# Issuing half of the output stores from GpSimd's queue, gating the token loads later, and planning the order anew, in a fused attention and feed-forward kernel

## The chip, the cores and the metric

The kernel runs on one core of a Trainium2 chip. The metric is the device time of one execution in microseconds (us). The profile's span, from the first to the last recorded instruction, is about 1.8 us shorter than that time. Every run has a state, fast or slow; ratios use fast runs only.

The engines are named as the profile does: PE is TensorE, PEld its weight loads, DVE VectorE, ACT ScalarE, POOL GpSimd, SP SyncE. SPq is SyncE's queue, which here does nothing but start transfers.

## The reference

```python
# attention: batch 4, 8 heads, sequence 768, head dimension 64; 8 global keys, window of 96
scores = q @ k.T / 8 + bias(slope per head, distance)     # masked outside window and globals
a = softmax(scores);  x = a @ v                           # -> 3072 tokens x 512
# feed-forward: d_model 512, d_ff 2048
h = x @ w_in
g = max(h, 0) + log1p(exp(-abs(h)))                       # softplus
out = g @ w_out                                           # 3072 x 512, float32
```

## The kernel before

The kernel cuts the 3072 tokens into 12 windows of 256. Each window's attention feeds a group of the feed-forward part: eight steps "mm1" (x times w_in, 8 matmuls of 128x256 each) and eight steps "mm2" (g times w_out, 4 matmuls of 128x512 each). Attention of later windows is laid between feed-forward steps of earlier ones, so that TensorE never runs dry.

No order is written down. Every piece of work is an operation with a rank; a planner inside the kernel simulates the engines and gives each engine, whenever it is free, the ready operation of lowest rank. A table RANKS shifts single ranks and BASE places whole blocks. The result is a list, and the instructions are then issued in its order:

```python
plan = pl.plan({"pe": 1.3, "dve": 4.5, "act": 2.1, "pool": 3.2, "sp": 0.7, "none": 0.0})
for op in plan:
    op.fn(op)
```

Each engine works through its own part of that list strictly in order, and waits at each entry for its data. The parts that the change touches are the stores, and the place of the token loads (q, k, v of a window, 1.5 MB together) in SyncE's queue:

```python
def store(g, ns):
    osb = state["osb", g, ns]                # 128 x 512 float32, three buffers
    t0 = W * g + P * ns
    nc.sync.dma_start(out[t0 : t0 + P, :], osb[:])
# ... two stores in each of eleven groups:
pl.add(f"store{g}_{ns}", "sp", 0.6, lambda op, g=g, ns=ns: store(g, ns), r + 1.5,
       after=[oc], frees=[(oc, "osb")], dma=(8, 110))
# ... loads of windows 4 to 11, in the plan only after a certain mm2 step:
for w in range(4, NWIN):
    for what, p in (("q", 0), ("k", 1), ("v", 3)):
        for o in loaded[w, what]:
            s = NSLOT * (w - 4) + p - PACE
            o.wait_for(mm2s[divmod(s, NSLOT)] if s >= 0 else landed["out3"])
```

SyncE's queue also carries the transposes of q and k (qT, kT) and of the attention's result (XT), some 1.2 us each. A q cast to bf16 runs on VectorE. The `wait_for` above holds only in the plan; on the chip a load waits for its buffer and its place in the queue.

The softmax here doesn't subtract the row's maximum and nothing guards it: scores larger than these inputs give would overflow.

Of the kernel before, what the change touches and what calls it, by code (L numbers as in the profile page):

```python
# [14 lines left out]


RANKS = {
    "Ck3.0": 33.6, "biasA.0": -11.6, "castv1.1": 17.3, "mm1_1_7.0": -3.6, "mm1_1_4.0": 27,
    "bias71.0": 46.2, "pv51.0": 12.4, "pv60.0": -37.2, "mm2_1_3.0": -35.8, "bias20.0": 10,
    "castv4.2": 2.9, "mm1_0_7.0": 16.2, "castv1.2": -20.8, "mm2_1_1.0": 14.7, "scores7.0": 7.8,  # L20
    "pv10.0": 15.8, "mm2_0_3.0": 15.4, "mm1_2_4.0": -4.3, "bias01.0": -10.4, "castk5.3": 11.8,
    "pv11.0": 13, "castv2.0": 11, "Fq1.0": -2, "castv4.3": -1.1, "mm1_1_2.0": -1.7,
    "sexp0_4.0": -6.9, "mm1_1_0.0": 2.2, "TX5.0": -6.8, "store0_1.0": -7.5, "Dq5.0": 0.9,
    "mm1_1_5.0": 3.1, "mm1_0_0.0": -3.2, "mm1_0_1.0": -3.5, "mm1_2_3.0": 2.6, "castv0.4": 4.3,
    "mm2_1_0.0": 12, "castv2.3": -2.5, "castv3.1": -1.2, "mm2_1_7.0": 3.4, "mm2_0_5.0": 14.2,
    "castv0.7": 8.8, "Dq4.1": -5, "castv0.3": -0.3, "castv0.5": 7.1, "mm1_2_2.0": -1.1,
    "mm2_1_4.0": -0.2, "mm1_0_5.0": -3.9, "castv0.1": -1.7, "castv3.3": -4.4, "castv0.2": -10.6,
    "castk4.1": 0.9,
}
HALVED = "q9 k9 q10 k10 v10 q11 k11 v11".split()  # L30
EARLY, MERGED, T_DMA, X_DMA = 4, 6, 4, 6
SP_ORDER = "Q01 K01 v0a Q23 K23 v0b v1 q2@in1 k2 v2 q3@in2 k3 v3"
POOL_ORDER = "in0@Q23 in1 out0 out1@q2 in2 in3 out2 out3"
PACE = 3
BASE = (-29.49, -25.67, -31.22, -11.48, -6.35, 14.94, 12.5, -27.18, 17.37, 24.12, 29.7, 32.51, 31.67, 35.31)


class Op:
# [206 lines left out]
def kernel(  # L245
# [11 lines left out]
    nc = tc.nc  # L257
    P = nc.NUM_PARTITIONS
# [327 lines left out]
    def mm1(g, p, turn):  # L586
        state["h", g, p] = h_ps[turn]
        hv = h_ps[turn][:].rearrange("p (j t) -> p j t", j=2)
        for j in range(2):
            fb = 2 * p + j  # L590
            for m in range(NM):
                nc.tensor.matmul(  # L592
                    hv[:, j, :],
                    w_in_bf[:, m, fb * P : fb * P + P],
                    XT[:, m, W * g : W * g + W],
                    start=(m == 0),
                    stop=(m == NM - 1),
                )

    def softplus_exp(g, p):  # L600
        e = tile_of(ffn, ("e", g, p // 2), [P, 2, 512], F32)

        nc.scalar.activation(  # L603
            e[:, p % 2, :].rearrange("p (a t r) -> p a r t", a=4, r=2),
            state["h", g, p][:].rearrange("p (a r t) -> p a r t", a=4, r=2),
            AF.Exp,
        )
# [55 lines left out]
        osb = tile_of(ffn, ("osb", g, ns), [P, DM], F32)  # L663
        copy_on[eng](osb[:], src)  # L664

    def store(g, ns):
        osb = state["osb", g, ns]
        t0 = W * g + P * ns
        nc.sync.dma_start(out[t0 : t0 + P, :], osb[:])

    def w_in_slice(s, waits):
        n_in = DFF // NS
# [36 lines left out]
    bias0 = const.tile([P, 2, 4, P], BF16, name="bias0")  # L709
    biasA = const.tile([P, 2, 8, P], BF16, name="biasA")  # L710
# [36 lines left out]
    def base(n):  # L747
        return BASE[n] if n < len(BASE) else 4.0 * n - 13.0

# [4 lines left out]
    def add_load(w, what, rank, after=(), hs=ALL, key=None, waits=()):  # L754
        nonlocal chain
        f = 0.5 if hs != ALL else 1.0
        dur, dma = 0.55 * f + 0.05, (64 * f, 28)
        takes = ((what + "32",),) if hs.start == 0 else ()
        o = chain = pl.add(
            f"load{what}{w}", "sp", dur, lambda op: load(w, what, hs, key, waits), rank,  # L760
            after=[*after, *(landed[x] for x in waits)], behind=[chain], takes=takes, dma=dma,
            slack=2.5 if w >= 4 else 0.0,
        )
        loaded.setdefault((w, what), []).append(o)
        return o
# [13 lines left out]
    def load_rest(w, rank, after=()):  # L779
        for i, what in enumerate("qkv"):  # L780
            for hs, _ in halves if what + str(w) in HALVED else whole:
                add_load(w, what, rank + 0.01 * i, after, hs)
# [36 lines left out]
    for w in range(4, NWIN):  # L819
        load_rest(w, base(2 * w) - 13.87 - PACE)  # L820

# [264 lines left out]
    for g in range(NGRP):  # L1086
        for p in range(NSLOT):
            r = NSLOT * g + p + {0: -1.04, 1: -0.28, 2: 0.38, 3: 1.0, 4: 1.55}.get(g, 0.0)
            m1 = mm1s[g, p] = pl.add(
                f"mm1_{g}_{p}", "pe", 0.875, lambda op, g=g, p=p: mm1(g, p, op.taken[0][1]), r,  # L1090
                after=[xdone[2 * g], xdone[2 * g + 1], landed_in[p * NS // NSLOT]],
                takes=(("H",),),
            )
            ex = pl.add(
                f"sexp{g}_{p}", "act", 0.63, lambda op, g=g, p=p: softplus_exp(g, p), r + 0.5,
                after=[m1], takes=(("e",),) if p % 2 == 0 else (), frees=[(m1, "H")],
            )
            if p % 2 == 1:
                lns[g, p // 2] = pl.add(
                    f"sln{g}_{p // 2}", "act", 1.06,  # L1100
                    lambda op, g=g, p=p: softplus_ln(g, p // 2), r + 0.9, after=[ex, prev_ex],
                    takes=(("g",),) if p == 1 else (), frees=[(prev_ex, "e")],
                )
            prev_ex = ex
        if g == NGRP - 1:
            before = None
            for part, (ns, cols, _) in enumerate(LAST):
                f = (cols.stop - cols.start) / DM
                for chunk in range(4):
                    before = pl.add(  # L1110
                        f"mm2l_{part}_{chunk}", "pe", 0.865 * f,
                        lambda op, part=part, chunk=chunk: mm2_last(part, chunk),
                        1000.0 + 4 * part + chunk,
                        after=[lns[g, chunk]], behind=[before],
                        takes=((LAST[part][2][0],),) if chunk == 0 else (),
                    )
                copies[part] = pl.add(
                    f"outl_{part}", "act" if part == 1 else "dve", 0.69 * f,
                    lambda op, part=part: out_last(op.on, part), 900.0,
                    after=[before], takes=(("osb",),),  # L1120
                )
            break
        for p in range(NSLOT):
            if g == 0:

                mm2s[0, p] = pl.add(
                    f"mm2_0_{p}", "pe", 0.865, lambda op, p=p: mm2_first(p, s_ps[1]), 2.19 * p + 2.01,
                    after=[lns[0, p // 2], landed_out[p * NS // NSLOT]], behind=[mm2s.get((0, p - 1))],
                    takes=(("S1",),) if p == 0 else (),
                )  # L1130
                continue
            ns, c = divmod(p, 4)
            mm2s[g, p] = pl.add(
                f"mm2_{g}_{p}", "pe", 0.865,
                lambda op, g=g, ns=ns, c=c: mm2_one(g, o_ps[:], ns, range(4 * c, 4 * c + 4)),
                NSLOT * (g + 1) + p + (-2.58 if g < 4 else 0.5),
                after=[lns[g, c], landed_out[c]], behind=[mm2s.get((g, p - 1))],
                takes=(("O",),) if c == 0 else (),
            )
        r = 2.6 + NSLOT if g == 0 else NSLOT * (g + 1) + 4.0  # L1140
        for ns in range(2):
            last = NSLOT - 1 if g == 0 or ns else 3
            oc = pl.add(
                f"oc{g}_{ns}", "dve", 0.69,
                lambda op, g=g, ns=ns: out_copy(
                    op.on, g, ns, o_ps[:] if g else o_first(ns, s_ps[1])
                ),
                r - 2.06 + 4 * ns, after=[mm2s[g, last], copies.get((g, 0))], takes=(("osb",),),
                frees=[(mm2s[g, 0], "S1")] * ns if g == 0 else [(mm2s[g, last - 3], "O")],
            )  # L1150
            if ns:
                oc.frees = [*oc.frees, (lns[g, 0], "g")]
            copies[g, ns] = oc
            pl.add(
                f"store{g}_{ns}", "sp", 0.6, lambda op, g=g, ns=ns: store(g, ns), r + 1.5,
                after=[oc], frees=[(oc, "osb")], dma=(8, 110),
            )

# [6 lines that stand above are left out]
# [42 lines left out]
```

## Time and profile before

| | before |
|---|---|
| median time | 219.18 us (218.71 to 219.36, 3 runs) |
| span of the profiled run | 217.1 us |
| TensorE busy / fillers | 208.3 us / 88 matmuls of zeros |
| stores | 23 of 256 KB on SyncE, 2.5 us from issue to landing |

TensorE is the bound. Lines from the costliest groups give line, engine, operation, tiles, shapes, count, then busy time and mean length, then the idle time ahead.

### The profile page before, as it was taken

How to read it: one execution, taken by the hardware profiler on the slowest of the kernel's cores; microseconds unless marked ns; L12 is line 12 of the kernel's file. 1: busy time of each engine (PE TensorE's matmuls, PEld its weight loads, DVE VectorE, ACT ScalarE, POOL GpSimd, SP SyncE). 2: the span in 40 equal slices, each digit the busy share in tenths (PEclk: the TensorE clock that was granted, in tenths of full speed). 3: DMA queues.
4: the chain of work that ended last, by engine and by line, in shares of the span. 5: the costliest groups of instructions: out<-in, count | busy, mean ns of one | idle time of the engine just before them, and what ended most of it. 6: DMA issues, size and time to landing. Idle time of an engine off the chain costs nothing.

```text
span 217.1 us, 5062 instructions
## 1 busy us (share of the span) xinstructions
PE 208.3 (96%) x2031; PEld 146.3 (67%) x2064; DVE 122.7 (57%) x261; ACT 153.7 (71%) x205; POOL 58.2 (27%) x113
## 2 busy tenths in 40 slices
PE   8899989999999999899999999999999999999994
PEld 7677766775766667577767767666766766676643
DVE  6878687278849677773555855545853753110020
ACT  3667859973896769768869669749669669766630
POOL 4652630014834360440441423221700000000000
PEclk9999999999999999999999999999999999999999
DMA  5999999999987977978999977969621211200112
GB/s 185 327 227 205 249 197 196 268 292 294 164 186 192 214 214 145 288 87 177 282 166 266 177 188 170 171 179 276 103 77 48 74 27 51 72 35 13 51 48 97
DMA packets 70583, 36.24 MB, mean 167 GB/s; under 512 B 28448, under 2 KB 67616, under 8 KB 70560
## 3 DMA queue, kind: packets, MB, share of 16 engines
q1 hardware_dynamic: 66192, 31.53, 63.8%
q0 software_dynamic: 4224, 4.19, 12.0%
q8 instruction: 16, 0.26, 0.6%
q10 hardware_dynamic: 144, 0.20, 0.3%
q14 instruction: 7, 0.06, 0.1%
HBM read 27.26 MB, written 6.29 MB: 155 GB/s over the span
## 4 chain that ended last, share of the span: by engine, by line
PE 83%; DMA 5%; DVE 4%; SPq 2%; issue 2%; POOL 1%; ACT 1%; DVEq 0%; POOLq 0%
PE h_ps L592 36%; PE o_ps L620 29%; DMA q<-in_q_dram 5%; PE s_ps L493 5%; PE x_ps L548 4%; PE s_ps L620 3%; PE s_ps L645 3%; DVE vb L402 1%; POOL vb L402 1%; SPq L441 1%; PE h_ps L419 1%; PE o_ps L732 1%; PE h_ps L570 1%; DVE xs L560 1%; SPq L582 1%
## 5 line engine op out<-in xcount | busy, mean ns | idle before, releaser
L592 PE MATMUL h_ps<-XT,w_in_bf 128*128 128x256 bf16 x768 | 96.0, 273 | 0.1
L603 ACT ACTIVATE e<-h_ps 128x512 f32<-128x512 f32 x96 | 58.7, 629 | 38.5 <-PE h_ps L592 38.1
L592 PEld LDWEIGHTS <-w_in_bf 128*128 128x128 bf16 x768 | 73.0, 98 | 19.1
L620 PE MATMUL o_ps<-w_out_bf,g 128*128 128x512 bf16 x294 | 75.5, 379 | 1.8 <-DVE osb L664 0.4
L611 ACT ACTIVATE g<-e 128x1024 bf16<-128x1024 f32 x48 | 50.5, 1055 | 0.6
L620 PEld LDWEIGHTS <-g 128*128 128x128 bf16 x352 | 32.1, 98 | 26.8 <-issue 0.4
L524 DVE TENSOR_TENSOR z<-s_ps,biasA 128x1024 f32<-128x1024 f32 x34 | 40.5, 1220 | 9.4 <-PE s_ps L493 8.0
L530 ACT ACTIVATE pb<-z 128x1024 bf16<-128x1024 f32 (+1 forms) x40 | 39.5, 986 | 7.6 <-DVE z L524 7.4
L402 POOL CAST kb<-k 64x512 bf16<-64x512 f32 x32 | 19.9, 621 | 48.5 <-DMA k<-in_k_dram 47.2
L402 POOL CAST vb<-v 64x512 bf16<-64x512 f32 (+1 forms) x40 | 24.4, 611 | 26.2 <-DMA v<-in_v_dram 24.3
L559 DVE RECIPROCAL rcp<-x_ps 128x4 f32<-128x4 f32 x47 | 8.5, 180 | 37.6 <-PE x_ps L548 34.5
L664 DVE COPY osb<-o_ps 128x512 f32<-128x512 f32 x20 | 13.7, 686 | 22.4 <-PE o_ps L620 22.2
L560 DVE TENSOR_TENSOR xs<-x_ps,rcp 128x256 bf16<-128x256 f32 x47 | 19.9, 424 | 1.7
L548 PEld LDWEIGHTS <-pb 128*128 128x128 bf16 x320 | 14.8, 97 | 3.5 <-issue 1.0
L548 PE MATMUL x_ps<-vb,pb 128*128 128x65 bf16 x312 | 15.8, 193 | 0.9 <-DVE xs L560 0.8
L493 PEld LDWEIGHTS <-kT 64*128 64x128 bf16 x288 | 8.3, 94 | 7.1 <-issue 6.4
L493 PE MATMUL s_ps<-qT,kT 64*128 64x128 bf16 x288 | 12.0, 218 | 0.6 <-DVE z L524 0.6
L471 DVE COPY vb<-vb 4x512 bf16<-4x512 bf16 (+1 forms) x36 | 11.7, 326 | 0.5
L393 DVE CAST qb<-q 128x1024 bf16<-128x1024 f32 x10 | 7.1, 712 | 8.3 <-DMA q<-in_q_dram 8.2
L732 PE MATMUL o_ps<-zeros 128*128 128x128 bf16 x88 | 9.3, 259 | 1.4 <-DVE zeros L687 1.0
L732 PEld LDWEIGHTS <-zeros 128*128 128x128 bf16 x88 | 7.3, 119 | 2.6 <-DVE zeros L687 1.0
L534 ACT ACTIVATE pb<-s_ps 128x1024 bf16<-128x1024 f32 (+1 forms) x8 | 7.3, 918 | 2.2 <-PE s_ps L493 2.2
(74 smaller groups left out, 96.9 us busy)
## 6 DMA issues: line engine op xcount, KB each, us to landing
out_dram<-osb SPq DMA_DIRECT2D x23, 256.0 KB, 2.5
q<-in_q_dram SPq DMA_DIRECT2D x9, 512.0 KB, 4.7
k<-in_k_dram SPq DMA_DIRECT2D x9, 512.0 KB, 6.9
v<-in_v_dram SPq DMA_DIRECT2D x9, 512.0 KB, 7.0
w_in_bf<-in_moe_w_in_dram POOLq DMA_DIRECT2D x4, 512.0 KB, 9.0
w_out_bf<-in_moe_w_out_dram POOLq DMA_DIRECT2D x4, 512.0 KB, 11.4
v<-in_v_dram SPq DMA_DIRECT2D x6, 256.0 KB, 4.5
q<-in_q_dram SPq DMA_DIRECT2D x6, 256.0 KB, 3.4
```

The source lines that it names most:

```text
L402: copy_on[eng](dst[64 * r : 64 * r + 64, hs, :], src)
L493: nc.tensor.matmul(s_t[:, 4 * sub + (lh // 2 if i == 0 else 2 * (lh // 2) + b), :], k_of(n - b, rows, m), q_of(n, rows, m), start=begin, s ...
L524: nc.vector.tensor_tensor(packed(n, z), rows_of(n, s_t), bias, ALU.add)
L530: nc.scalar.activation(pb[:, 0:nr, :], z[:, 0:nr, :], AF.Exp, scale=1.0 / root_d)
L548: nc.tensor.matmul(xv[:, lh, :], pb[:, 2 * j + b, :], vb_of(n - b)[:, h, :], start=b == 0, stop=b == 1,)
L560: nc.vector.tensor_tensor(xs[:, 4 * half : 4 * half + 4, :], xv[:, :, 0:D], rcp[:][:, :, None].to_broadcast([P, 4, D]), ALU.mult,)
L592: nc.tensor.matmul(hv[:, j, :], w_in_bf[:, m, fb * P : fb * P + P], XT[:, m, W * g : W * g + W], start=(m == 0), stop=(m == NM - 1),)
L603: nc.scalar.activation(e[:, p % 2, :].rearrange("p (a t r) -> p a r t", a=4, r=2), state["h", g, p][:].rearrange("p (a r t) -> p a r t", a ...
L611: nc.scalar.activation(gt[:, 4 * c : 4 * c + 4, :].rearrange("p a t -> p (a t)"), state["e", g, c][:].rearrange("p a t -> p (a t)"), AF.Ln ...
L620: nc.tensor.matmul(dst, state["g", g][:, fb, ns * P : ns * P + P], w_out_bf[:, fb, :], start=(fb == 0), stop=(fb == NFB - 1),)
L664: copy_on[eng](osb[:], src)
L732: nc.tensor.matmul(o_ps[:, 0:P], zeros[:], zeros[:])
```

## The change

The intent: twelve of the stores are to leave SyncE's queue, so that they no longer stand ahead of loads and transposes; the loads are gated later; and since the planner's input has changed, ranks and bases were searched anew.

```diff
 RANKS = {
-    "Ck3.0": 33.6, "biasA.0": -11.6, "castv1.1": 17.3, "mm1_1_7.0": -3.6, "mm1_1_4.0": 27,
-    ... (51 entries)
+    "mm1_1_4.0": 26.1, "bias71.0": 63.7, "bias20.0": 9.6, "castk5.3": 11.8, "Dq5.0": 0.9,
+    ... (43 entries)
 }
-HALVED = "q9 k9 q10 k10 v10 q11 k11 v11".split()
+HALVED = "q8 k8 v8 q9 k9 v9 q10 k10 v10 q11 k11 v11".split()
-PACE = 3
-BASE = (-29.49, -25.67, -31.22, -11.48, -6.35, 14.94, 12.5, -27.18, ...)
+PACE = 0
+STORES = 6
+BASE = (-29.37, -38.43, -34.65, -17.24, 5.3, 14.23, -7.79, -35.22, ...)
...
-    def store(g, ns):
+    def store(eng, g, ns):
         osb = state["osb", g, ns]
         t0 = W * g + P * ns
-        nc.sync.dma_start(out[t0 : t0 + P, :], osb[:])
+        start = nc.gpsimd.dma_start if eng == "pool" else nc.sync.dma_start
+        start(out[t0 : t0 + P, :], osb[:])
...
-                f"store{g}_{ns}", "sp", 0.6, lambda op, g=g, ns=ns: store(g, ns), r + 1.5,
+                f"store{g}_{ns}", *(("pool", 0.8) if g < STORES else ("sp", 0.6)),
+                lambda op, g=g, ns=ns: store(op.on, g, ns), r + 1.5,
```

## The prediction

> **What bounds the kernel now.** I read the busy table and the slice chart first, then the table of stretches, then the list of waits of TensorE, then the chain of waits in order of time around the largest hole.
>
> ```profile
> PE 208.3 (96%) x2031; PEld 146.3 (67%) x2064; DVE 122.7 (57%) x261; ACT 153.7 (71%) x205; POOL 58.2 (27%) x113
> ...
> PEclk9999999999999999999999999999999999999999
> ```
>
> TensorE is busy 208.3 of 217.1 us at full clock; the next engine, ScalarE, has 71%. So TensorE is the bound, and the time can fall only by what TensorE idles or wastes: 217.1 - 208.3 = 8.8 us. Where that idle time lies is in the table of stretches (columns: stretch, length, busy time and count of TensorE, weight loads, VectorE, ScalarE, GpSimd, then granted clock, DMA share, GB/s):
>
> ```profile
> 0.00:25.00 25.00, 22.61 (x296) 18.03 (x301) 18.83 (x68) 16.37 (x23) 11.40 (x31) 1.00 1.02 245
> 25.00:75.00 50.00, 49.00 (x490) 34.41 (x497) 34.11 (x64) 37.36 (x51) 16.55 (x28) 1.00 1.13 221
> 75.00:90.00 15.00, 13.60 (x153) 9.92 (x153) 10.95 (x20) 12.03 (x16) 4.51 (x9) 1.00 0.82 204
> 90.00:210.00 120.00, 118.94 (x1063) 81.26 (x1081) 57.84 (x109) 87.50 (x117) 25.71 (x48) 1.00 0.59 129
> 210.00:217.10 7.10, 4.10 (x35) 2.64 (x33) 0.98 (x2) 0.48 (x1) 0.00 (x0) 1.00 0.21 74
> ```
>
> Length minus busy gives the idle time: 2.39 us in the first 25 us (first loads), 1.00 from 25 to 75, 1.40 from 75 to 90, 1.06 over the long regular part, 3.00 at the end (last copies and stores). The start and end hang on the first loads and the last store. Ahead of 90 us the list of waits names three real stalls:
>
> ```profile
> PE x_ps L548 <- DVE xs L560: 0.8, 1, 0.8
> PE s_ps L493 <- DVE z L524: 0.6, 1, 0.6
> PE o_ps L620 <- DVE osb L664: 0.4, 1, 0.4
> ```
>
> They sum to 1.8 us, each one event. The largest, at 89 us, is followed back in the chain of waits in order of time (start, length, what):
>
> ```profile
> 80.10 1.22 SPq L582
> ...
> 81.41 1.75 SPq L441
> ...
> 83.22 4.57 DMA q<-in_q_dram
> ...
> 88.49 0.19 DVE rcp L559
> ```
>
> SyncE worked through transposes, only then issued the q load at 83.22; the load took 4.57 us; VectorE, which takes its work in order, stood before the q cast until 87.8, so the softmax division behind it came late, and TensorE's probabilities-times-V matmuls waited 0.80 us. Why the queue was late shows in SyncE's own timeline and waits:
>
> ```profile
> 69.01 4.02 SPq L441 DMA_TRANSPOSE qT<-qb  x1
> 73.08 1.54 SPq L669 DMA_DIRECT2D out_dram<-osb  x3
> ```
>
> ```profile
> SPq L669 <- DVE osb L664: 31.4, 11, 6.5
> ```
>
> Three stores stood ahead of those transposes for 1.54 us, and over the whole run SyncE stood 31.4 us in 11 waits for a store's result to be copied out of PSUM. Everything behind waited too.
>
> **What the Trainium skill says.** "DMA: Bandwidth & Descriptors", section "Issuing engines are not separate DMA queues": all queues end on the same 16 engines, and another issuing engine "will only save the time on the sequencer it takes to initiate the DMA". The trace agrees as far as it goes: the weight loads of GpSimd's queue took 9.0 to 11.4 us to land while SyncE's loads ran too. So I expect no bandwidth from the move, only SyncE's time. The same page, "Anatomy of one DMA — SWDGE (gpsimd) path", fits a GpSimd DMA as 2.0 us + bytes/436e3; for 256 KB that is an estimate of 2.6 us, beside a median of 2.5 us that SyncE's stores took. Landing time is therefore no reason for or against. "Perfetto Trace Analysis", section "DMA Instruction — SWDGE (GPSIMD)", says that the recorded end of such an issue is the end of descriptor writing, not of the transfer; the trace has these rows at 747 to 926 ns, on GpSimd itself. "SBUF — State Buffer", section "SBUF: two separate sides", warns that VectorE operations in a two-port mode keep GpSimd from writing descriptors; no row of this trace isolates that, though a v cast of 0.61 us median once took 0.96 us.
>
> **The change part by part.**
> 1. Twelve of 22 whole-tile stores leave SyncE. Recorded issues there run from 0.33 to 1.72 us, median 0.377: 12 x 0.38 = 4.5 us of issue, plus a good part of the 31.4 us of waiting. None of it lies on TensorE directly; it counts only where a transpose or load behind it is late, and in this trace that is the 0.80 us stall, perhaps the 0.4 us one (a copy into osb that held TensorE's next output group).
> 2. GpSimd gains them: 12 x 0.82 us (median of its eight weight loads) = 9.8 us as an upper estimate, since a store has 128 rows and a weight slice 512. GpSimd idles 73% of the span, so there is room; but its queue is in order too. A store that waits for osb holds the next k or v casts, and casts that wait for a load hold the store (the longest such wait now is 15.2 us).
> 3. The gate is three steps later. In the built instruction streams the loads wait only for earlier DMA lanes and free buffers, not for the matmul step. The gate is thus only a place in SyncE's order. It puts the loads after more transposes; a load issued at 83.22 that was already late could get later. Against that, between the v load of window 6 and the q load of window 7 the streams have ten other SyncE entries before (three of them stores) and six after. At roughly 1.2 us per transpose and 0.5 us per store that is 1.5 to 3 us sooner, relative to its neighbours, more than the 0.80 us stall.
> 4. The new order. Comparing the streams, TensorE's matmuls are the same 1976 in both apart from fillers, 88 before and 84 after; the order differs mainly before the fifth group, and later little. Four fillers at about 56 ns spacing are 0.2 us. The q, k, v loads of window 8 and v of window 9 are now halved, which lets casts start sooner but adds four issues.
>
> Sum: 1.8 us of named stalls plus 0.2 us of fillers is at most 2.0 us to gain. I chose to credit three quarters of the stalls, 1.35 us, because the order was searched for exactly this, plus the 0.2, and take off 0.1 us for a new short wait: 219.18 - 1.35 - 0.2 + 0.1 = 217.7 us. That is a gain of 0.7%.
>
> **Rivals.**
> - *Hidden anyway.* SyncE's freed time is slack and only one stall hung on it; the reordering moves the others about. For it: the regular part from 90 to 210 us has just 1.06 us of idle in spite of all those SyncE waits. Then 218.6 to 219.4 us. This is the closest rival.
> - *GpSimd becomes the late one.* A store waiting for osb delays k casts, then the k transposes, then scores, and TensorE stalls. For it: GpSimd is already in the chain (four v casts at 76.7 to 79.3 us lead to the late transposes), and the stores come right there. Against it: 58.2 + 9.8 us is 31% of the span, and most casts wait for a load rather than for GpSimd. If two or three windows each lose half a microsecond, 219.5 to 221 us.
> - *Loads late.* The later gate makes q casts on VectorE wait longer; each microsecond of such waiting in the dense part costs up to as much. With one or two events like the one at 88 us: plus 0.8 to 1.6 us, again about 219 to 220.5.
> - *The start improves too.* If the first groups start earlier, part of the 2.39 us of idle and 84 x 56 ns = 4.7 us of fillers in the first 25 us goes. The first 81 fillers stand in the same places in both streams and the first loads are unchanged, so I allow 0.5 us at most: 217.2.
>
> **Range and chances.** All stalls gone and a little of the start gives about 216.3; a gain wholly given back and a new stall gives 219.5. Over 2% faster means below 214.8, a gain of 4.4 us: more than double the stalls named, so 2%. Over 2% slower means 4.4 us of new TensorE idle, which needs a repeated stall in each window: 3%. Within 2%: 95%.
>
> **What would show it.** Right: SyncE's waits for osb fall from 31.4 us to under half; GpSimd shows twelve store issues of at most 0.9 us; idle TensorE from 75 to 90 us falls from 1.40 to below 0.8; the regular part stays near 1.06; the stores' landing stays near 2.5 us. Wrong: new entries in TensorE's waits that lead back through a k or v cast to a store on GpSimd, or through a q cast to a late load; or the same work with TensorE's stalls merely moved. It would also be wrong if the startup changed by over 1 us, which I gave no credit.

## More of the kernel before

```profile
L620 PE MATMUL o_ps<-w_out_bf,g 128*128 128x512 bf16 x294 | 75.5, 379 | 1.8 <-DVE osb L664 0.4
L620 PEld LDWEIGHTS <-g 128*128 128x128 bf16 x352 | 32.1, 98 | 26.8 <-issue 0.4
```

Every matmul has a weight load of its own. There are 352 loads, yet only 294 matmuls are recorded into o_ps and another 28 into s_ps: 30 records are missing (33 over all kinds). Where the record of a matmul is missing, the trace shows idle time.

## The result, and the profile after

The changed kernel took 217.91 us (median of 4 runs, 217.75 to 218.05) beside 219.27 us (4 runs) before. The ratio is 0.9941, with a 95% interval of 0.9919 to 0.9963. A ratio here is the mean time of one kernel's fast runs over the mean of the other's in the same rounds, so it is not quite the ratio of the medians.

The page and the table of stretches after, the counterparts of those in the prediction (same columns; the last stretch ends with the span):

```profile
PE 210.3 (97%) x2060; PEld 146.1 (68%) x2060; DVE 122.0 (56%) x258; ACT 156.4 (72%) x208; POOL 65.2 (30%) x125
```

```profile
0.00:25.00 25.00, 22.32 (x291) 17.60 (x292) 19.03 (x67) 15.58 (x21) 11.23 (x31) 1.00 1.03 245
25.00:75.00 50.00, 49.92 (x497) 34.35 (x495) 33.33 (x61) 40.69 (x55) 18.16 (x31) 1.00 1.10 233
75.00:90.00 15.00, 15.00 (x164) 10.56 (x162) 10.45 (x19) 12.27 (x17) 6.89 (x12) 1.00 0.90 167
90.00:210.00 120.00, 120.00 (x1092) 81.50 (x1089) 58.64 (x112) 87.43 (x116) 28.97 (x52) 1.00 0.54 129
210.00:216.00 6.00, 3.05 (x30) 2.05 (x27) 0.58 (x2) 0.48 (x1) 0.00 (x0) 1.00 0.25 87
```

From 75 to 90 us TensorE is now busy throughout, where it idled 1.40 us. But look at the first line and at the fourth, the regular stretch. In the first 25 us it is busy 22.32 us, 0.29 us less than before. And in the regular stretch it has gone from 118.94 to 120.00 us busy, though both kernels do the same there. The count of matmul records explains the fourth line: 2060 of 2060 this time, none missing, against 2031 of 2064. The 1.06 us are 20 gaps of 0.05 us each, and a later profile of the changed kernel itself (the first control of experiment 7), with 34 records missing, shows 20 such gaps again, 1.16 us. So the 1.06 us that the prediction read as idle was no idle time at all.

Busy time is thus a poor yardstick between these two traces. The weight loads are complete in both, so I use them: **lost time** at a moment is the elapsed time minus the back-to-back time of all real matmuls whose weights have been loaded by then (spacings read off in unstalled stretches: 0.1093 us for 128x256, 0.2158 for 128x512, 0.1625 for 128x384, 0.109 for the 128x256 bias, 0.056 for a 128x128 transpose, 0.035 for a scores matmul, 0.030 for a 65-column one; fillers count as nothing). The real work sums to 197.7 us in both kernels.

| lost time at | 10 us | 25 us | 35 us | 75 us | 90 us | 210 us |
|---|---|---|---|---|---|---|
| before | 7.76 | 11.29 | 12.46 | 13.13 | 14.90 | 16.24 |
| after | 8.03 | 12.20 | 12.53 | 13.59 | 13.84 | 15.16 |
| after minus before | +0.27 | +0.91 | +0.07 | +0.46 | -1.06 | -1.08 |

The steps are good to some 0.2 us, the length of a matmul. The final difference, 1.08 us, agrees with the spans (217.1 - 216.0 = 1.1 us). By stretches: the start to 25 us **loses** 0.91 us, 25 to 75 us gains 0.45 us, 75 to 90 us gains 1.52 us, and the rest nothing. The gain from 25 to 75 us lies all before 35 us (0.84 us), where the stall of 0.6 us stood (at 30.64 us); from 35 to 75 us the changed kernel loses 0.39 us more than the other, and no single wait in its list explains that.

The waits of TensorE after, in full apart from those under 0.5 us:

```profile
PE o_ps L732 <- DVE zeros L687: 1.0, 1, 1.0
PE h_ps L591 <- DVE rcp L558: 0.7, 1, 0.7
PE o_ps L732 <- ACT k_first L385: 0.5, 1, 0.5
```

The first and the last were there before. All three stalls that the prediction names are gone, and there is a new one of 0.7 us: the first feed-forward matmuls, near 18.6 us.

What freed the stage near 89 us is in the list of waits of the other engines. First before, then after (what waited, for what: us in total, times, longest):

```profile
DVE qb L393 <- DMA q<-in_q_dram: 8.2, 4, 4.1
POOL kb L402 <- DMA k<-in_k_dram: 47.2, 7, 10.3
```

```profile
DVE qb L392 <- DMA q<-in_q_dram: 1.4, 1, 1.4
POOL kb L401 <- DMA k<-in_k_dram: 13.7, 5, 5.8
POOL out_dram L669 <- DVE osb L663: 16.8, 6, 6.7
SPq L669 <- DVE osb L663: 27.1, 8, 6.5
```

VectorE stood 8.2 us at q casts whose load had not landed; now 1.4 us. (One q cast moved to GpSimd, where it waits 8.7 us; no wait of TensorE in this profile follows from it.) SyncE's own time at stores hardly fell, from 31.4 to 27.1 us: most of it belongs to the late groups, whose stores still go through SyncE. The list of SyncE's waits before, up to 133 us (the twelve stores that move) and from there on, shows it:

```profile
SPq L669 <- DVE osb L664: 2.6, 3, 1.1
SPq L669 <- DVE osb L664: 28.8, 8, 6.5
```

So the move could save 2.6 us of this waiting at most. And SyncE's timeline after, in the same place as the one that the prediction shows:

```profile
79.98 1.22 SPq L440 DMA_TRANSPOSE kT<-kb  x1
81.25 0.57 SPq L350 DMA_DIRECT2D q<-in_q_dram  x1
```

The q load of window 7 leaves at 81.25 us, 2.0 us sooner than before, and its cast is planned behind other work of VectorE (it runs at 88.82 us, when the data is there). The q load of window 6 left later than before, at 67.72 in place of 66.40 us, as the later gate would have it, and no stall followed.

The stores themselves, from the issues (KB each, median us from issue to landing) and from the source line (ns minimum/median/maximum of the issue):

```profile
out_dram<-osb POOLq DMA_DIRECT2D x12, 256.0 KB, 4.5
out_dram<-osb SPq DMA_DIRECT2D x11, 256.0 KB, 2.1
```

```profile
L669 POOL DMA_DIRECT2D out_dram<-osb x12: 540/542/822, 50.0 to 131.5; - x12
```

They cost GpSimd 0.54 us each, and take twice as long to land as those that SyncE issues. But the two sets do not run at the same time of the kernel. Taken alone, the same twelve stores had a median of 4.2 us on SyncE in the kernel before, and 3.8 and 3.5 us on SyncE in the changed kernel's order (experiment 2); on GpSimd in that order it is 4.5, 4.1 and 5.0 us in three profiles (means: 4.1 us in both on SyncE, 4.3 to 4.5 us on GpSimd). So most of the difference between 4.5 and 2.1 us is the part of the kernel in which they run, and not the queue.

### The profile page after: what moved, and what is told of

The parts are those of the page before. It is cut to its first block, busy times and chain, and to the rows that moved or that the text cites. A ratio compares the mean times of both kernels' runs of the same rounds, so it can differ in the third digit from the quotient of the medians.

```text
span 216.0 us, 5102 instructions
## 1 busy us (share of the span) xinstructions
PE 210.3 (97%) x2060; PEld 146.1 (68%) x2060; DVE 122.0 (56%) x258; ACT 156.4 (72%) x208; POOL 65.2 (30%) x125
## 4 chain that ended last, share of the span: by engine, by line
PE 91%; DMA 3%; DVE 2%; ACT 1%; SPq 1%; issue 0%
PE h_ps L591 40%; PE o_ps L619 32%; PE s_ps L492 6%; PE x_ps L547 5%; DMA q<-in_q_dram 3%; PE s_ps L644 3%; PE s_ps L619 3%; PE o_ps L732 1%; PE h_ps L418 1%; PE s_ps L477 1%; DVE vb L401 1%; DVE kb L370 0%; SPq L358 0%; PE o_ps L644 0%; PE x_ps L544 0%
## 5 line engine op out<-in xcount | busy, mean ns | idle before, releaser
L619 PE MATMUL o_ps<-w_out_bf,g 128*128 128x512 bf16 x320 | 79.6, 379 | 0.0
L401 POOL CAST vb<-v 64x512 bf16<-64x512 f32 (+1 forms) x39 | 23.4, 601 | 5.9 <-DMA v<-in_v_dram 3.9
L401 POOL CAST kb<-k 64x512 bf16<-64x512 f32 x32 | 20.6, 644 | 15.0 <-DMA k<-in_k_dram 13.7
L461 POOL COPY kT<-kT 128x32 bf16<-128x32 bf16 x12 | 2.5, 209 | 36.2 <-PE s_ps L492 26.7
L669 POOL DMA_DIRECT2D out_dram<-osb x12 | 6.8, 568 | 18.7 <-DVE osb L663 16.8
L732 PE MATMUL o_ps<-zeros 128*128 128x128 bf16 x84 | 8.7, 261 | 1.4 <-DVE zeros L687 1.0
```

Source lines behind the costliest of these rows:

```text
L401: copy_on[eng](dst[64 * r : 64 * r + 64, hs, :], src)
L619: nc.tensor.matmul(dst, state["g", g][:, fb, ns * P : ns * P + P], w_out_bf[:, fb, :], start=(fb == 0), stop=(fb == NFB - 1),)
```

## The experiments

Two kinds of run have to be told apart. Changing a constant makes the planner plan everything anew, so such a run changes the order everywhere. To hold the order still, I edited the finished list instead, or only the engine that issues; then every compute engine keeps its order to the instruction (checked on the built streams, and the traces agree). Times are medians of six runs, with the ratio to the kernel before and its 95% interval.

**1. The queue alone.** The order before, stores of six groups from GpSimd.

```diff
     def store(g, ns):
-        nc.sync.dma_start(out[t0 : t0 + P, :], osb[:])
+        start = nc.gpsimd.dma_start if g < 6 else nc.sync.dma_start
+        start(out[t0 : t0 + P, :], osb[:])
```

> The order of the kernel before is kept instruction for instruction on every engine; only the twelve stores of the first six groups go out through GpSimd's queue in place of SyncE's. Theory Q (SyncE's queue): the stores ahead of the transposes made the window-7 q load late, so the 0.8 us stall near 89 us goes and perhaps the 0.4 us one near 77: 218.0 to 218.6 us, q load issued 1.5 to 2 us sooner than 83.2. Rival O (order): the queue alone buys nothing, 219.0 to 219.5 us, and the three stalls of TensorE stay. Rival G (GpSimd late): stores hold k casts, over 219.8 us.

218.88 us, ratio 0.9987 (0.9966 to 1.0008): no clear gain, just under the range that the rival O gave. The trace shows both theories half right. SyncE's q load of window 7 left at 81.26 us, and the stall near 89 us shrank: lost time rose by 0.26 us from 80 to 90 us, against 1.23 us before. But a new wait took its place:

```profile
PE s_ps L493 <- DMA qT<-qb: 1.3, 1, 1.3
```

The chain of waits in order of time, ahead of it, and GpSimd's timeline there:

```profile
67.36 1.33 SPq L351
...
68.73 9.18 DMA qT<-qb
...
78.05 0.63 PE s_ps L493 x16
```

```profile
68.51 1.60 POOL L670 DMA_DIRECT2D out_dram<-osb  x3 [0.32 <-issue]
```

A q transpose stands right behind the three loads of window 6 (1.5 MB) in SyncE's queue. Three stores (768 KB) now start on GpSimd at 68.5 us, at the same moment; in the kernel before they stood behind the transpose, at 73.08 us. The transpose lands 9.18 us after issue and TensorE waits 1.3 us. In the kernel before the same transpose was issued at 69.01 us, landed after 7.17 us, and the same scores ran at 76.69 us without a wait. The v load just ahead of the transpose was slowed as much: it landed after 10.09 us in place of 8.06.

**2. The order alone.** The changed kernel's order, all stores from SyncE, tried on two chips (the second time beside the changed kernel).

```diff
-        start = nc.gpsimd.dma_start if eng == "pool" else nc.sync.dma_start
+        start = nc.sync.dma_start
```

> The order of the changed kernel is kept on every engine; only the twelve stores go back to SyncE's queue, at the places where the plan has them. Theory Q: the late loads come back, 218.6 to 219.4 us. Rival O: the time stays at 217.8 to 218.2 us, that is the new order alone makes the gain and the queue is irrelevant.

> The changed kernel's order with all stores back on SyncE, again, now beside the changed kernel. In the first trial its profiled run lost no more TensorE time than the changed kernel, yet its six runs spread over 1.5 us (218.18 to 219.72). If the queue move buys steadiness: again a spread over 1 us and a mean 0.5 to 1.2 us above the changed kernel of this batch. If that spread was chance: within 0.3 us of the changed kernel.

First 218.79 us, ratio 0.9989 (0.9963 to 1.0014); then 218.87 us, ratio 0.9977 (0.9948 to 1.0006), with a mean 0.59 us above the changed kernel of the same batch. So the order alone is not the gain either. The profile of the first trial was one of its better executions (218.38 us) and lost no more TensorE time than the changed kernel. That of the second (219.44 us) shows what the stores do in SyncE's queue:

```profile
65.67 0.53 SPq L669 DMA_DIRECT2D out_dram<-osb  x1
66.29 2.54 SPq L440 DMA_TRANSPOSE kT<-kb  x2
68.88 1.26 SPq L440 DMA_TRANSPOSE qT<-qb  x1
70.20 1.42 SPq L350 DMA_DIRECT2D q<-in_q_dram  x1
```

The q load of window 6 leaves at 70.20 us; in the changed kernel it left at 67.72 us. VectorE and TensorE, in their timelines:

```profile
75.76 0.70 DVE L392 CAST qb<-q 128x1024 bf16<-128x1024 f32 x1 [2.19 <-DMA q<-in_q_dram]
```

```profile
77.05 0.40 PE L547 MATMUL x_ps<-vb,pb 128*128 128x65 bf16 x8 [0.96 <-DVE xs L559]
```

VectorE stands 2.19 us before the q cast and TensorE loses 0.96 us. It is the mechanism of the old stall at 89 us, one window earlier. The expectation that the queue move would buy steadiness fell: the changed kernel itself spread over 1.45 us in that batch (217.61 to 219.06).

**3. One late load alone.** The kernel before, stores on SyncE, with the q load of window 7 five transposes sooner in SyncE's queue, and nothing else moved; tried twice.

```diff
+    i = next(k for k, op in enumerate(plan) if op.name == "loadq7")
+    j = next(k for k, op in enumerate(plan) if op.name == "castq6")
+    j = max(j, next(k for k, op in enumerate(plan) if op.name == "store1_1"))
+    ... (a print)
+    plan.insert(j + 1, plan.pop(i))
     for op in plan:
         op.fn(op)
```

> The kernel before with one thing moved: the q load of window 7 stands five transposes sooner in SyncE's queue, the stores stay where they are. If the late q load is the cause of the largest stall (TensorE 0.8 us near 89 us, 1.06 us of lost work there): the stall is gone and the time is 218.1 to 218.5 us. If VectorE's order or the transposes are the cause, the stall stays or moves and the time is 219.0 to 219.6 us.

> The kernel before with the q load of window 7 five transposes sooner, again. If that one late load is what the whole change amounts to: 0.5 to 1.1 us below the kernel before, within 0.4 us of the changed kernel. If the changed kernel's other differences count: 0.5 us or more above the changed kernel.

First 218.36 us, ratio 0.9973 (0.9948 to 0.9998); then 218.49 us, ratio 0.9957 (0.9924 to 0.9991). VectorE's q cast in the kernel before:

```profile
87.88 0.69 DVE L393 CAST qb<-q 128x1024 bf16<-128x1024 f32 x1 [1.21 <-DMA q<-in_q_dram]
```

In the first trial, SyncE's q load and then VectorE:

```profile
75.96 0.58 SPq L351 DMA_DIRECT2D q<-in_q_dram  x1
```

```profile
86.60 0.68 DVE L393 CAST qb<-q 128x1024 bf16<-128x1024 f32 x1
87.20 0.18 DVE L559 RECIPROCAL rcp<-x_ps 128x4 f32<-128x4 f32 x1
```

The load left at 75.96 us, the cast ran at 86.60 us without a wait, the division followed at once, and TensorE's stall near 89 us is gone. Lost time at 90 us was 13.82 us (before: 14.90; changed kernel: 13.84) and 15.16 us at 210 us, as in the changed kernel. The stall is gone in the second trial's profile too. The late load was the cause of the largest stall, and mending it alone gives part of the gain. How large a part the traces cannot say: in both trials the profiled run was the fastest of the six. In the second trial the mean was 0.16 us above the changed kernel's, with a spread of 2.3 us, so how much of the whole it gives stays loose: the two ratios make it 0.6 and 0.9 us, each with an interval of more than 0.5 us to either side.

**4. Both halves, by hand.** Experiment 1 plus one move: the q transpose ahead of the loads of window 6, as the later gate has it in the changed kernel.

```diff
+    at = {op.key: k for k, op in enumerate(plan) if hasattr(op, "key")}
+    plan.insert(at["loadq6.0"], plan.pop(at["Dq5.0"]))
```

> The order of the kernel before, the twelve stores on GpSimd's queue, and one q transpose of window 5 put ahead of the three loads of window 6 in SyncE's queue, as the later gate does in the changed kernel. Theory (both parts are needed): with the stores alone the transpose landed 9.2 us after issue behind those loads and TensorE waited 1.3 us near 78 us; with the transpose first that wait is gone, the stall near 89 us stays away, and the time is 217.9 to 218.4 us, the gain of the whole change. Rival (the gain is in the searched order of the compute engines): 218.7 to 219.4 us, with the wait moved on once more.

218.76 us, ratio 0.9976 (0.9949 to 1.0004). The wait for qT is gone, as expected: its issue moved to 66.76 us and the scores ran at 78.06 us without a wait. The time is a miss, and lies in the range of the rival. The profiled run was the slowest of the six (219.56 us), had lost 1.1 us more than the kernel before by 25 us, at the first loads and casts, and waited 0.34 us near 89 us again. So the contention in experiment 1 is confirmed by its cure; that these two moves make up the change is not.

**5. Old ranks, and the old gate, with the rest of the change.** Both plan everything anew.

```diff
-RANKS, BASE of the changed kernel          (first run)
+RANKS, BASE of the kernel before
-PACE = 0                                   (second run)
+PACE = 3
```

> The changed kernel with the ranks and bases of the kernel before: stores on GpSimd, gate three steps later and halved loads are kept, the order is planned anew from the old ranks. If the stores and the gate make the gain: 217.6 to 218.4 us, and the first 25 us lose 0.4 to 0.9 us less than in the changed kernel. If the searched ranks are needed for it: 218.8 to 220.5 us, with stalls of TensorE between 30 and 100 us.

> The changed kernel with its gate three steps earlier again, planned anew. If the later gate is needed so that the transposes stand ahead of the loads in SyncE's queue: 218.6 to 220 us, with a wait for a transposed q or k on TensorE between 60 and 100 us. If the gate is immaterial beside the stores: 217.7 to 218.2 us.

Old ranks: 220.48 us, ratio 1.0072 (1.0042 to 1.0102). Old gate: 220.17 us over all six runs, one of them (223.03 us) slow; ratio of the five fast ones 1.0048 (1.0002 to 1.0093). One of these five took 222.49 us; without it the ratio would be 1.002. So old ranks are clearly slower than the kernel before, and the old gate is slower than the changed kernel (219.23 us at least, beside 217.91 at most in the same batch), but not clearly slower than the kernel before. With old ranks TensorE's lost time rose by 4.0 us between 80 and 90 us (before: 1.2 us; changed kernel: 0.2 us); two new waits of 1.1 and 0.9 us are behind ScalarE, and in that stage of this run the granted clock fell (the last three numbers are clock, DMA share and GB/s):

```profile
85.00:90.00 5.00, 4.14 (x23) 2.73 (x21) 3.72 (x6) 2.33 (x3) 0.54 (x1) 0.66 0.62 145
```

The two waits are half of the 4.0 us; the rest lies in this stage of slow clock, and what lowered the clock is open. The clock is not what makes the kernel slower as a whole: four of its six runs had a mean clock of 0.998 or more, and took 220.0 to 220.8 us. With the old gate the longest new wait is 0.7 us for a transposed result (XT), landed 3.62 us after issue; the expected wait for q or k did not appear. Neither run tells what its constant is worth by itself. They tell that ranks, gate and stores fit each other, and that a searched order does not survive a change of one of them.

**6. The start mended.** The changed kernel, with the XT copy that the first feed-forward matmuls need put ahead of a v cast and two small copies on VectorE.

```diff
+    at = {op.key: k for k, op in enumerate(plan) if hasattr(op, "key")}
+    late = [plan[at["gv2.1"]], plan[at["castv1.2"]]]
+    ... (an assert)
+    i = at["norm20.0"]
+    plan[i + 1 : i + 1] = late
+    for op in late:
+        plan.remove(op)
```

The reason is in VectorE's timeline of the changed kernel and TensorE's below it:

```profile
17.03 1.27 DVE L401 CAST vb<-v 64x512 bf16<-64x512 f32 x2
18.33 0.46 DVE L470 COPY vb<-vb 4x256 bf16<-4x256 bf16 x2
18.82 0.42 DVE L578 COPY XT<-h_ps 128x512 bf16<-128x512 bf16 x1
```

```profile
19.39 0.81 PE L591 MATMUL h_ps<-XT,w_in_bf 128*128 128x256 bf16 x6 [0.75 <-DVE rcp L558]
```

The bracket names the division, but the copy into XT ended at 19.24 us and is what these matmuls read; the name of a releaser is inferred.

> The changed kernel with one repair in its start: on VectorE the copy that frees the first feed-forward matmuls is put ahead of a v cast and two copies of v rows, so that TensorE does not wait 0.7 us near 18.5 us. If what TensorE loses in the start counts to the end: 217.0 to 217.4 us. If the loads and transposes set the time of the stage near 76 us anyway, the start's gain is given back there: 217.7 to 218.2 us, as the changed kernel.

> The changed kernel with the start repaired on VectorE, again beside the changed kernel. TensorE lost 0.5 us less in its profile; two of its six runs were 0.8 us slower than the other four. If the repair holds: mean 0.2 to 0.6 us below the changed kernel. If the start's gain is mostly given back: within 0.15 us of it.

First 217.42 us, ratio 0.9923 (0.9894 to 0.9953); then 217.18 us, ratio 0.9903 (0.9876 to 0.9929). In its trace the copy ran at 17.64 us and the matmuls at 18.32 us:

```profile
18.32 1.05 PE L591 MATMUL h_ps<-XT,w_in_bf 128*128 128x256 bf16 x8
```

Lost time at 25 us was 11.50 us in both profiled runs, in place of 12.20. At 210 us it was 14.67 us in the first, 0.5 us less than the changed kernel, and 15.32 us in the second, where a weight load landed late (TensorE waited 0.6 us for w_out). Over both batches, all on one chip, the twelve runs average 217.48 us, the changed kernel's twelve 217.97 us; the difference is 0.49 us, with a 95% interval of 0.11 to 0.86 us from the spread of the runs. But that difference comes almost all from one batch: the means differ by 0.07 us in the first and by 0.90 us in the second, where the control was slow (expected were 0.2 to 0.6 us). That it beats the kernel before is clear; that it beats the changed kernel is likely, and not shown.

**7. Controls.** The changed kernel again, in the batches of the runs above.

> The changed kernel itself, as a control beside the next three and to see how far its runs spread: 217.7 to 218.4 us, ratio to the kernel before 0.993 to 0.997.

> The changed kernel as the control of this batch: 217.4 to 218.1 us, all six runs within 0.6 us of each other as in its ten runs so far (217.46 to 218.05).

217.67 us, ratio 0.9923 (0.9899 to 0.9948), and 218.18 us, ratio 0.9950 (0.9919 to 0.9981). With the first result that makes three ratios between 0.992 and 0.995. The third control broke the expectation of a spread under 0.6 us. Executions of one kernel differ by 2 us and more here, fast ones alone (the kernel before: 218.40 to 220.70 us in one batch); lost time at 10 us alone ranged from 7.69 to 8.31 us over the profiles, before any order differs.

## Why the prediction was right

The time (217.91 us beside 217.7 us predicted) is within the range, and the sign and size of the gain are right. The main chain was read rightly. The terms of the sum are partly wrong and cancelled, so that the total came this close is in part luck. (The lower end of the range, 216.3 us, does not follow from the prediction's own terms: 219.18 less 1.8 for the stalls, 0.2 for fillers and 0.5 for the start is 216.7.)

- **What bounds the kernel.** Right: the time followed TensorE's lost time, 1.08 us of it for 1.1 us of span. Wrong in one reading: "1.06 over the long regular part" was idle time made of missing records.
- **The three stalls, credited at 1.35 us.** Mis-sized, on the low side: all three went, and the stages with them, 25 to 75 and 75 to 90 us, gained 0.45 + 1.52 = 1.97 us of lost time. The stall of 0.6 us at 30.64 us is not gone merely because TensorE comes there later: it stays away with the start mended too (experiment 6).
- **The start, credited with 0.2 us for fillers.** This term failed. Four fillers fewer did not mean an earlier start; the start lost 0.91 us. Some 0.3 us of that was there at 10 us, where the orders do not yet differ, and is the run's own. (The prediction would have called itself wrong had the start changed by over 1 us; 0.91 us is close.) The rest goes with the order: with the changed order unmended lost time at 25 us was 11.72 to 12.20 us in five profiles, and 11.50 us with the copy moved. A filler stands where the plan expects a hole; its count says nothing of holes that the plan did not expect. By 35 us, with the stall at 30.64 us gone, the two kernels were level again (+0.07 us). The rival "The start improves too" had the wrong sign.
- **0.1 us for a new short wait.** It was 0.7 us, and lies in the start, not where stores or loads were expected to cause it.
- **The queue.** The chain was read rightly: stores ahead of transposes, transposes ahead of the q load, VectorE behind the load, TensorE behind VectorE. The first experiment shows it by taking the stores away, the third by mending the load alone. "1.5 to 3 us sooner" was 2.0 us. But "SyncE's waits for osb fall to under half" failed: 27.1 of 31.4 us stayed. The prediction counted "a good part" of the 31.4 us for the twelve stores; their part was 2.6 us. Their issues, in turn, took 8.2 us in the profile before and not 4.5 us: the median of 0.38 us over all stores is lower than that of these twelve.
- **GpSimd's cost.** 0.54 us per store in place of 0.82, 6.8 us in all in place of 9.8. The rival "GpSimd becomes the late one" did not come about; its casts found shorter waits than before.
- **"Landing time is therefore no reason for or against."** Half right. The median of 2.5 us over all stores hid that these twelve took 4.2 us on SyncE already; on GpSimd's queue they took 4.5 us, so "the stores' landing stays near 2.5 us" failed as a sign, but not by the move. What failed is "I expect no bandwidth from the move, only SyncE's time": started sooner, in the first experiment, three stores ran beside a v load and a transpose, and these two took 2.0 us longer to land than before. The rivals did not include this one: a transfer that overtakes another because it changed queues.
- **"Hidden anyway", the closest rival.** It describes the two halves taken alone well (0.9987 for the queue, 0.9989 and 0.9977 for the order), but not the whole. The stall near 89 us goes with either half: lost time from 80 to 90 us rose by 0.26 us with the queue alone and by less than 0.5 us with the order alone. In the profiles each half alone has a wait elsewhere: 1.3 us near 78 us, and 0.24 and 0.96 us near 76 us.

What stays open: how much of the gain each half carries. No run has one part alone with an order that fits it, and the runs spread too widely to split a gain of 1.3 us finely.

## What to carry to other kernels

Where engines work in order, look for the one late transfer at the head of a chain rather than at sums of queue time: of 31.4 us of waiting in SyncE's queue, 28.8 us lay late in the kernel, where nothing was gained, and moving one load sooner took away the largest stall, of 0.80 us. Moving transfers to another queue also changes which transfer comes first on the shared engines, so look for what they now overtake. And before reading idle time off a trace, compare the count of matmuls with the count of weight loads.

## What the Trainium skill lacked or had wrong

- "DMA: Bandwidth & Descriptors", section "Issuing engines are not separate DMA queues", says that transfers of all queues interleave on the same 16 engines and that another issuing engine saves only issue time. It does not say that the move changes which transfer starts first. The runs show this effect: three stores of 256 KB that left SyncE's queue started 4.6 us sooner (68.51 in place of 73.08 us), beside loads and a transpose, and that transpose landed 9.18 us after issue in place of 7.17, with a 1.3 us wait of TensorE. Putting the transpose ahead of the loads took that wait away.
- The same page, section "Anatomy of one DMA — SWDGE (gpsimd) path": the fit of 2.0 us + bytes/436e3 gives an estimate of 2.6 us for 256 KB; under this kernel's traffic the stores of GpSimd took 4.5 us (median of twelve), in the first experiment 5.1 us. The same twelve on SyncE took 4.2 us. A figure for a busy core is missing there.
- No page gives the cost of an issue on GpSimd by rows: 0.54 us for a store of 128 rows of 2 KB, 0.75 to 0.93 us for the weight loads here.
- "Perfetto Trace Analysis", section "Identifying the Most-Contended Engine", rightly warns of matmul busy time, but does not say that records can be missing: 33 of 2064 here, which made 1.06 us of idle time in a stretch where a complete trace of the same work has none.
